# A quarter of the queries takes its softmax maximum from raw scores in SBUF, in a one-core attention and gated-ReLU kernel

## The chip, the cores and the metric

The kernel runs on one core of one Trainium2 chip. Its time is the device time in microseconds (us) of that core; the number compared is the median of several executions.

## The reference

Two blocks read the same input `x` (2048 tokens by 448) and are mixed by one gate per token. All values are float32.

```python
qkv = (x @ wqkv).reshape(B, S, 3, H, Dh)          # H = 16 heads, Dh = 28
scores = einsum("bhqd,bhkd->bhqk", q, k) * (Dh ** -0.5)
a = einsum("bhqk,bhkd->bhqd", softmax(scores, axis=-1), v) ... @ wo
gate = relu(einsum("bsd,df->bsf", x, W_gate)); up = einsum("bsd,df->bsf", x, W_up)
b = einsum("bsf,fd->bsd", gate * up, W_down)       # F = 1792
g = sigmoid((x * gate_w).sum(-1, keepdims=True))
return g * a + (1 - g) * b
```

## The kernel before

The program has three stages. Up to about 144 us it makes q, k and v of all heads (`qk`, L352; `vproj`, L370), with the first products of attention set among them. From there to about 1051 us it runs attention, head by head, with gate and up products of the second block (`gu_mm`, L526) laid among the attention products to fill TensorE. The rest finishes the second block (`down`, L789) and the output projection (`wout`, L744).

A large matmul here streams 512 columns, and float32 operands are split into a high part and a remainder, so that a product of 448 terms is eleven matmuls (`TERMS`). The split is made by `split_f`: ScalarE copies the high part (L130), and GpSimd subtracts it to get the remainder (`pool_low`, L139). Every split chunk of gate and up weights costs ScalarE three copies and GpSimd four subtractions, and the chunk after it is fetched from HBM by a DMA on SyncE's queue (`fetch_f`, L233), which may go only when the buffer of the chunk just split is free.

In attention the scores of a head are made with keys on partitions and 512 queries on the free axis (`scores`, L217), since the product with V needs them that way. ScalarE takes each of these tiles from PSUM through Exp into SBUF (L219). The maximum over keys that is subtracted inside the exponent cannot be read off such a tile, since it would run over partitions. So the kernel computes the scores a second time, with queries on partitions (`smax`, L191), and VectorE reduces each of these tiles to one column (L192). These are called maxima products below: 64 a head, 1024 in all. When the 64 are done, `smax_end` transposes the 16 columns on TensorE (L199), splits them, and two DMAs put them into two spare rows of Q (L207), against which K holds -1. The score matmul of the next head then subtracts its own maximum.

The products with V (`pv`, L560) come in a block of their own at the end of each round: four column-tiled matmuls for each of the key tiles that the round finished, accumulated in one PSUM bank; VectorE then takes the bank to SBUF (L564 for the first block of a head, L566 for later ones, which add). Row sums ride along as a column of ones in V; `row_sums`, `spread` and `normalise` (L574, L582, L586) turn them into a factor and scale the head's output.

The order of instructions is written out by hand. Each string in `ROUNDS` is one round, a letter for each matmul: `s` a score product, `m` a maxima product, `x` a gate or up product (`S`, `M`, `N` are the same with another PSUM bank). What is issued after a round's letters is in the loop's tail: the last gate and up matmuls, the ReLU on ScalarE (L539), the product of gate and up on VectorE (`hidden`, L542), its DMA on GpSimd's queue (L548), the weight splits, `normalise`, and `pv`. Each engine works through its own instructions in this order and waits where it must; eight PSUM banks hold the products until ScalarE or VectorE has read them, so a bank not yet read stops TensorE.

## Time and profile before

| what | before |
| --- | --- |
| median of 3 runs | 1260.16 us (1260.05 to 1260.63) |
| profiled execution, first to last instruction (span) | 1258.2 us |
| PE busy | 1252.8 us |
| VectorE (DVE) busy | 854.8 us |
| ScalarE (ACT) busy | 748.4 us |
| GpSimd (POOL) busy | 374.3 us |

The page gives the profiled execution by its span; no time of its own beside that is listed for it, and the median of the runs is 2.0 us more than the span. PE is TensorE, SPq is SyncE's DMA queue. Overlapping instructions of one engine are counted once in busy time, while the mean in nanoseconds is of one instruction alone, so the pace of instructions that follow each other closely is shorter than that mean. The chain of waits goes back from the last instruction to what released it; in it a matmul has only the time until the next begins, so it shows the pace.

### The profile page before, as it was taken

The numbers are of one execution on the slowest core, as the hardware profiler recorded it, in microseconds if no ns is written. First come the engines' busy times: TensorE is split into PE (matmuls) and PEld (weight loads), VectorE is DVE, ScalarE is ACT, GpSimd is POOL, SyncE is SP. The second block draws the span as 40 slices with busy tenths as digits, with TensorE's granted clock in tenths as the row PEclk, the third lists the DMA queues.
The fourth block names the chain that finished last, engine by engine and source line by source line (L and its number), as shares of the span: only waits on it lengthen the run. The fifth ranks groups of instructions, "written<-read, shape, count | busy, mean of one in ns | idle before, by whom it ended". The sixth has DMA issues, their size and how long they took to land.

```text
span 1258.2 us, 18270 instructions
## 1 busy us (share of the span) xinstructions
PE 1252.8 (100%) x6687; PEld 919.1 (73%) x6687; DVE 854.8 (68%) x1363; ACT 748.4 (59%) x1424; POOL 374.3 (30%) x569
## 2 busy tenths in 40 slices
PE   9999999999999999999999999999999999999998
PEld 6888866677666676666766667766667666899997
DVE  6599767687777797776977778877778224663342
ACT  6312767686666776666866667766677773312121
POOL 4222222312334123423133331134222444651020
PEclk9999999999999999999999999999999999999999
DMA  8955453144245314241544323142431226634432
GB/s 302 315 206 209 117 155 99 50 106 104 60 115 173 81 43 121 68 113 44 130 121 127 100 80 90 43 122 67 114 94 50 84 85 208 223 110 138 145 106 79
DMA packets 54113, 151.00 MB, mean 120 GB/s; under 512 B 10304, under 2 KB 17416, under 8 KB 49160
## 3 DMA queue, kind: packets, MB, share of 16 engines
q1 hardware_dynamic: 36632, 100.44, 29.2%
q0 software_dynamic: 16960, 48.94, 11.0%
q8 instruction: 52, 0.85, 0.3%
q10 hardware_dynamic: 432, 0.46, 0.1%
q14 instruction: 37, 0.30, 0.1%
HBM read 104.16 MB, written 46.03 MB: 119 GB/s over the span
## 4 chain that ended last, share of the span: by engine, by line
PE 99%; DMA 0%; SPq 0%; DVE 0%; ACT 0%; issue 0%
PE b L526 22%; PE b L191 19%; PE b L217 19%; PE b L560 18%; PE b L789 11%; PE b L352 5%; PE b L370 3%; PE b L744 3%; DMA xr<-x 0%; PE b L199 0%; SPq L304 0%; DVE X L136 0%; DVE y L795 0%; ACT X L130 0%; SPq L384 0%
## 5 line engine op out<-in xcount | busy, mean ns | idle before, releaser
L192 DVE TENSOR_REDUCE mx<-b 128x1 f32<-128x512 f32 x1024 | 646.5, 685 | 51.2 <-PE b L191 50.7
L219 ACT ACTIVATE P<-b 128x512 f32<-128x512 f32 x840 | 467.1, 599 | 160.8 <-PE b L217 139.0
L526 PE MATMUL b<-X,wg 128*128 128x512 f32 (+1 forms) x1232 | 415.3, 394 | 0.0
L191 PE MATMUL b<-K,Q 128*128 128x512 f32 x1024 | 389.6, 391 | 0.0
L217 PE MATMUL b<-Q,K 128*128 128x512 f32 x1024 | 389.3, 390 | 0.0
L526 PEld LDWEIGHTS b<-X,wg 128*128 128x128 f32 (+1 forms) x1232 | 220.2, 187 | 53.8 <-issue 9.3
L217 PEld LDWEIGHTS b<-Q,K 128*128 128x128 f32 x1024 | 192.3, 188 | 46.3 <-issue 6.7
L191 PEld LDWEIGHTS b<-K,Q 128*128 128x128 f32 x1024 | 192.4, 188 | 44.3 <-issue 5.9
L560 PE MATMUL b<-P,V 128*32 128x512 f32 x1680 | 188.2, 593 | 0.0
L548 POOL DMA_DIRECT2D h_d<-h x56 | 31.3, 558 | 405.4 <-DVE h L542 354.9
L139 POOL TENSOR_TENSOR wg<-wgr,wg 128x384 fp32r<-128x384 f32 x200 | 143.2, 731 | 10.4 <-DVE wg L133 2.0
L560 PEld LDWEIGHTS b<-P,V 128*32 128x32 f32 x1680 | 52.7, 110 | 120.0 <-issue 116.8
L789 PE MATMUL b<-WD,hh 128*128 128x448 f32 x672 | 138.5, 365 | 0.0
L219 ACT ACTIVATE V<-b 128x512 f32<-128x512 f32 x184 | 105.0, 599 | 48.8 <-PE b L217 42.3
L789 PEld LDWEIGHTS b<-WD,hh 128*128 128x128 f32 x672 | 126.2, 188 | 10.3
L130 ACT ACTIVATE hh<-hr 128x512 fp32r<-128x512 f32 x56 | 35.3, 631 | 124.7 <-PE b L789 120.2
L136 DVE TENSOR_TENSOR hh<-hr,hh 128x512 fp32r<-128x512 f32 x56 | 45.7, 815 | 66.4 <-ACT hh L130 66.3
L352 PE MATMUL b<-X,W 128*128 128x512 f32 x308 | 83.1, 393 | 0.1
L566 DVE TENSOR_TENSOR os<-b,os 128x512 f32<-128x512 f32 x16 | 11.1, 692 | 86.5 <-PE b L560 86.5
L352 PEld LDWEIGHTS b<-X,W 128*128 128x128 f32 x308 | 57.4, 188 | 14.5 <-DVE X L136 1.6
L130 ACT ACTIVATE wg<-wgr 128x384 fp32r<-128x384 f32 x156 | 62.2, 490 | 7.9 <-DMA wgr<-wgu 3.9
L575 POOL DMA_DIRECT2D l_d<-rs x16 | 8.9, 559 | 186.2 <-DVE rs L574 186.2
(74 smaller groups left out, 665.6 us busy)
## 6 DMA issues: line engine op xcount, KB each, us to landing
wgr<-wgu SPq DMA_DIRECT2D x55, 512.0 KB
K<-qk_d SPq DMA_DIRECT2D x64, 224.0 KB
Q<-qk_d SPq DMA_DIRECT2D x64, 224.0 KB
h_d<-h POOLq DMA_DIRECT2D x56, 256.0 KB, 2.7
hr<-h_d SPq DMA_DIRECT2D x56, 256.0 KB
qk_d<-st POOLq DMA_DIRECT2D x21, 512.0 KB, 4.2
x_d<-X POOLq DMA_DIRECT2D x6, 1024.0 KB, 5.4
X<-x_d SPq DMA_DIRECT2D x24, 256.0 KB
```

What stands on the lines that cost most here:

```text
L130: nc.scalar.activation(dst, src, AF.Copy)
L136: nc.vector.tensor_tensor(dst, src, f32(high), op=OP.subtract)
L139: nc.gpsimd.tensor_tensor(dst, src, f32(high), op=OP.subtract)
L191: nc.tensor.matmul(ps, Q[h][:, u * P:(u + 1) * P], K[h % 3][:, c * TB:(c + 1) * TB], start=True, stop=True)
L192: nc.vector.tensor_reduce(MX[h][:, 4 * u + c:4 * u + c + 1], ps, axis=AX.X, op=OP.max)
L217: nc.tensor.matmul(ps, K[h % 3][:, kt * P:(kt + 1) * P], Q[h][:, j * TB:(j + 1) * TB], start=True, stop=True)
L219: nc.scalar.activation(PT[i][:, j], ps, AF.Exp, scale=SCALE)
L352: nc.tensor.matmul(ps, W[:, a, c * P:(c + 1) * P], xf(tb, b), start=(n == 0), stop=(n == NT - 1))
L370: nc.tensor.matmul(ps[:, :VC], xf(tb, b)[:, t * P:(t + 1) * P], W[:, a, 2 * D:2 * D + VC], start=(n == 0), stop=(n == NT - 1))
L526: nc.tensor.matmul(ps, WS[i][rows, s, a], xf(i // NF, b)[rows], start=(n == 0), stop=(n == NT - 1))
L560: nc.tensor.matmul(po[32 * j:32 * j + 32], V[:, h // 4 % 2, i % NK, h % 4], p[:, j], start=(i == i0), stop=(i == i0 + ni - 1))
L789: nc.tensor.matmul(ACC[i // NF][t][:, :D], HH[i][:, a, t * P:(t + 1) * P], WD[:, f, b], start=(f == 0 and n == 0), stop=(f == NF - 1 and n ...
```

## The change

For heads 1 to 15 the last 512 of the 2048 queries no longer get maxima products: 48 of 64 remain for each of these heads (head 0 keeps its 64). The score products of that quarter are made a head earlier, without a maximum in Q's spare rows, and go raw into SBUF (`raw_scores`: ScalarE, Copy instead of Exp). Sixteen raw tiles of a head are folded by VectorE with an elementwise maximum into one running tile (`raw_max`, 15 for each head). `raw_top` finds the maximum over partitions: a 32x32-block transpose, a reduction, four small copies, a second reduction and transpose, all on VectorE; then a DMA writes 512 numbers to HBM and a second reads them back to all 128 partitions, both on SyncE's queue. `raw_less` subtracts that tile from each of the 16 raw tiles (GpSimd; VectorE in two late rounds), and `raw_exp` is the Exp, from SBUF to SBUF on ScalarE.

The raw tiles need room for 24 tiles of 128x512. They take it from V: all of V is written to HBM at the start (`v_d`), and each head's V comes back in a DMA of its own (`load_v`). A round is now always eight key tiles, half a head, so there are 32 rounds, and `pv` always covers eight key tiles, in bank 3. The strings name banks outright (`m0` is a maxima product in bank 0) and have new letters: `r` a raw score product, `d` a `raw_max`, `e` a `raw_exp`. In the strings AA the eight `r` have no `d`, so that the `raw_max` of such a round stand in the loop's tail. Even rounds (first half of a head) are of the kind AA, odd ones BB (two chunks of gate and up) or BA (one chunk). 54 chunks instead of 50 are worked off in attention, and 96 instead of 112 maxima products stand in the first stage.

The strings were all rewritten; one of each shows the form.

```diff
-TWO = ("msMxsxmsxmNxxsmMsxxsmSsxmxsMNxmxsmxsxMSsmxmsxMSmssxmMxSmssxmSxMsxsmxmsxMsxmsxmsMxsmxsxmsxmsxxsmxsmxs"
-       "xmsxmxsxmxsmxsxxmsmshh")
-ROUNDS = [(FIRST, 4)] + [(TWO, 4), (THREE, 4), (ONE, 4)] * 7 + [(LATE, 6), (FINAL, 6)]
+AA = ("xm0s1r2xm6s7xxm3s1xm0xs2r6xm7s3xxm1s0xr2em6xs7xm3s1exm0xs2xr7em3s1xxm0s2exm7xs3xr1em0s2xxm7s3exm1s0x"
+      "r2xem3s1xm0xes2xm3s1xr0xm2s3xm1xs0xm2s3xr1m0s2xm1xs0xm2xs1x")
+BA = ("xm0s1r2m6s7xm3s1xm0s2r6xem7s3m1s0xr2dem6s7xm3s1xem0s2dxm6s7xem3s1m0s2xm7es6xm1s3xr2em0xr6s7m3em1s2xd"
+      "s0m6s3exm7s1xm2s0xr6r3xm7s1r2m0s6xm7xs1s0m2")
+ROUNDS = [FIRST, SECOND, AA, BB, AA, BA, AA, BA] + [AA, BB, AA, BB, AA, BA, AA, BA] * 2
+ROUNDS += [AA, BA, AA, BA, AY, BY, AZ, BZ]
...
+    def rows_of(h):
+        return NK if h == 0 else NK - 4
+    MAXIMA = [(h, u, c) for h in range(H) for u in range(rows_of(h)) for c in range(4)]
...
+    def raw_scores(i, ps, late=False):
+        h, kt = divmod(i, NK)
+        own = prob(i, 3)
+        nc.tensor.matmul(ps, K[h % 3][:, kt * P:(kt + 1) * P], Q[h][:, 3 * TB:], start=True, stop=True)
+        if late:
+            nc.vector.tensor_copy(own, ps)
+        else:
+            nc.scalar.activation(own, ps, AF.Copy)
+    def raw_max(i):
+        run = piece(RUN)
+        nc.vector.tensor_tensor(run, prob(i, 3), run if i % NK > 1 else prob(i - 1, 3), op=OP.max)
+    def raw_top(h):
+        run, turned = piece(RUN), piece(TURNED)
+        nc.vector.transpose(turned, run)
+        top, four = run[:, :16], run[:32, 16:80].rearrange("p (a b) -> p a b", a=4)
+        square, row = run[:32, 96:128], run[:32, 128:160]
+        nc.vector.tensor_reduce(top, turned.rearrange("p (b i) -> p b i", i=32), axis=AX.X, op=OP.max)
+        for a in range(4):
+            nc.vector.tensor_copy(four[:, a], top[32 * a:32 * a + 32])
+        nc.vector.tensor_reduce(square[:, :16], four.rearrange("p a b -> p b a"), axis=AX.X, op=OP.max)
+        nc.vector.transpose(row, square)
+        nc.sync.dma_start(mr_d[h], row[:16])
+        nc.sync.dma_start(piece(TOP), mr_d[h].rearrange("b c -> (b c)").rearrange("(a t) -> a t", a=1).to_broadcast([P, TB]))
+    def raw_less(i, engine):
+        own = prob(i, 3)
+        engine.tensor_tensor(own, own, piece(TOP), op=OP.subtract)
+    def raw_exp(i):
+        own = prob(i, 3)
+        nc.scalar.activation(own, own, AF.Exp, scale=SCALE)
...
+    def load_v(h):
+        VH[h] = fe.tile([P, NK, 32], F32, name=f"v_{h}", tag="v", bufs=2)
+        nc.sync.dma_start(VH[h], v_d[h])
...
+        if r % 2 == 0:
+            small_things(h)
+            if h:
+                for i in range(i0, i0 + 8):
+                    raw_less(i, nc.gpsimd)
...
+        while top < raw:
+            raw_max(top)
+            top += 1
+        if r % 2 and raw == NK * (h + 2):
+            raw_top(h + 1)
+            top += 1
+        if r % 2 == 0 and h:
+            ahead = "e" not in ROUNDS[r + 1]
+            for i in range(i0 + 8, i0 + NK):
+                raw_less(i, nc.vector if ahead else nc.gpsimd)
+                if ahead:
+                    raw_exp(i)
         while summed:
             normalise(summed.pop())
-        for a in {i0, max(i0, (i0 + ni) // NK * NK)}:
-            n = min(i0 + ni, (a // NK + 1) * NK) - a
-            if n > 0:
-                pv(a, n, ps_p if late else ps_m)
-        i0 += ni
+        pv(i0, 8, banks[3])
```

Three places show what the tail of a round now holds. The first is VectorE at the end of a round with a `normalise`, before the change; L542 is `hidden`, L586 `normalise`, L564 the bank of the products with V, and L192 the first maximum of the next round.

```order
L195 TENSOR_REDUCE m_2323<-mx_1887 128x16
L542 TENSOR_TENSOR h_2334<-b_74,rl_2332 128x512
L542 TENSOR_TENSOR h_2342<-b_76,rl_2340 128x512
L586 TENSOR_TENSOR os_1728<-os_1728,rb_2262 128x512
L564 COPY os_2415<-b_71 128x512
L192 TENSOR_REDUCE mx_2421<-b_72 128x1
```

VectorE at the end of an even round after the change. L611 is `hidden`, L267 `raw_max` (its running tile lies in V's space), L659 `normalise`, L637 the bank of the products with V, L229 the maxima of the next round.

```order
L611 TENSOR_TENSOR rl_2432<-b_74,rl_2432 128x512
L611 TENSOR_TENSOR rl_2439<-b_76,rl_2439 128x512
L267 TENSOR_TENSOR V<-P_1072,P_1030 128x512
L267 TENSOR_TENSOR V<-P_1114,V 128x512
L267 TENSOR_TENSOR V<-P_1149,V 128x512
L267 TENSOR_TENSOR V<-P_1197,V 128x512
L267 TENSOR_TENSOR V<-P_1248,V 128x512
L267 TENSOR_TENSOR V<-P_1280,V 128x512
L267 TENSOR_TENSOR V<-P_1331,V 128x512
L659 TENSOR_TENSOR os_1982<-os_1982,rb_2328 128x512
L637 COPY os_2506<-b_72 128x512
L229 TENSOR_REDUCE mx_2378<-b_69 128x1
```

Seven `raw_max`, each of which reads two tiles in SBUF, now stand between `hidden` and the bank of the products with V.

GpSimd around the end of the same even round, from the DMAs of `spread` (L655) on; before the change the remainders (L139) were followed by the DMAs of `normalise` alone.

```order
L139 TENSOR_TENSOR wg_2346<-wgr_2021,wg_2346 128x384 x2
L139 TENSOR_TENSOR wg_2346<-wgr_2021,wg_2346 64x128 x2
L139 TENSOR_TENSOR wg_2356<-wgr_2031,wg_2356 128x384 x2
L139 TENSOR_TENSOR wg_2356<-wgr_2031,wg_2356 64x128 x2
L588 DMA o_d<-os_1728 28x512 x4
L139 TENSOR_TENSOR mh_2419<-mr_2418,mh_2419 16x128
```

After the change; L617 is the DMA of the gate and up product, L149 the remainders of a weight chunk, L285 `raw_less`, L661 the DMAs of `normalise`.

```order
L655 DMA rb_2328<-l_d_103 32x512 x4
L617 DMA h_d_2435<-rl_2432 128x512
L617 DMA h_d_2442<-rl_2439 128x512
L149 TENSOR_TENSOR wg_2444<-wgr_2181,wg_2444 128x384 x2
L149 TENSOR_TENSOR wg_2444<-wgr_2181,wg_2444 64x128 x2
L285 TENSOR_TENSOR V<-V 128x512 x8
L661 DMA o_d<-os_1982 28x512 x4
L149 TENSOR_TENSOR mh_2510<-mr_2509,mh_2510 12x128
```

Eight subtractions of 128x512 have come in behind the remainders, and they stand beside the `raw_max` of VectorE.

SyncE's queue at the end of an odd round, after the change: L303 fetches weight chunks, L280 and L281 are the two DMAs of `raw_top`, L626 is `load_v`, L205 to L212 are K and Q of a later head.

```order
L303 DMA wgr_2181<-wgu 128x1024
L303 DMA wgr_2191<-wgu 128x1024
L280 DMA mr_d_87<-V 16x32
L281 DMA V<-mr_d_87 128x512
L626 DMA v_2239<-v_d 128x512
L205 DMA K_128<-qk_d 28x2048 x4
```

The two DMAs of `raw_top` are new, and they stand behind the fetches that wait for GpSimd's remainders.

216 lines of the change are left out of this document (113 added, 103 removed).

## The prediction

> **What bounds the kernel now.** I read the page's busy times first, then the chain of waits, then the groups, and last the timeline of one round's end.
>
> ```profile
> PE 1252.8 (100%) x6687; PEld 919.1 (73%) x6687; DVE 854.8 (68%) x1363; ACT 748.4 (59%) x1424; POOL 374.3 (30%) x569
> ...
> PE 99%; DMA 0%; SPq 0%; DVE 0%; ACT 0%; issue 0%
> ```
>
> TensorE is the bound without a gap, so a matmul taken out is time saved at its pace, as long as nothing new stops TensorE. The chain gives the paces:
>
> ```profile
> by line: PE b L526 21.8%; PE b L191 18.6%; PE b L217 18.6%; PE b L560 17.7%; PE b L789 10.8%; PE b L352 5.4%; PE b L370 2.9%; PE b L744 2.8%; DMA xr<-x 0.4%; PE b L199 0.3%; SPq L304 0.1%; DVE X L136 0.1%; DVE y L795 0.1%; ACT X L130 0.1%;
> ...
> 316.59 8.72 PE b L560 x80
> ...
> 394.92 9.58 PE b L560 x88
> 404.50 0.21 PE b L199
> ...
> L191 PE MATMUL b<-K,Q 128*128 128x512 f32 x1024 | 389.6, 391 | 0.0
> ```
>
> 18.6% of 1258.2 us over 1024 maxima products is 0.2285 us each (the group's mean of 391 ns overlaps the next matmul). The 80 matmuls of L560 are ten key tiles, 0.87 us each, so eight take 6.97 us. In that block TensorE hands nothing to VectorE and ScalarE, which catch up. What they do there is the question, so here is the block from 394.92 on, with VectorE, GpSimd, ScalarE and SyncE's queue in turn.
>
> ```profile
> 394.71 0.22 DVE L195 TENSOR_REDUCE m<-mx 128x16 f32<-128x64 f32 x1
> 395.45 1.29 DVE L542 TENSOR_TENSOR h<-b,rl 128x512 f32<-128x512 f32 x2 [0.52 <-ACT rl L539]
> 396.66 0.68 DVE L586 TENSOR_TENSOR os<-os,rb 128x512 f32<-128x512 f32 x1
> 404.62 0.69 DVE L564 COPY os<-b 128x512 f32<-128x512 f32 x1 [7.28 <-PE b L560]
> ...
> 396.44 1.14 POOL L548 DMA_DIRECT2D h_d<-h  x2 [5.24 <-DVE h L542]
> 397.60 6.03 POOL L139 TENSOR_TENSOR wg<-wgr,wg 128x384 fp32r<-128x384 f32 x8
> ...
> 394.81 1.09 ACT L539 ACTIVATE rl<-b 128x512 f32<-128x512 f32 x2
> 395.77 2.39 ACT L130 ACTIVATE wg<-wgr 128x384 fp32r<-128x384 f32 x6
> ...
> 400.66 3.32 SPq L233 DMA_DIRECT2D wgr<-wgu  x2
> ```
>
> VectorE sits idle for 7.28 us of it, while GpSimd works until 403.63. Two 128x512 VectorE instructions fill 1.29 us, a pace of 0.60; two ScalarE ones 1.09, a pace of 0.48.
>
> **What two SBUF inputs cost beside GpSimd.** `raw_max` reads two SBUF tiles. Attention has few such instructions now, so I looked where the last stage has them: VectorE and GpSimd about 1102 us, then about 1067 us.
>
> ```profile
> 1102.22 0.69 DVE L136 TENSOR_TENSOR hh<-hr,hh 128x512 fp32r<-128x512 f32 x1
> 1102.83 1.35 DVE L133 CAST WD<-wdr 128x448 fp32r<-128x448 f32 x1
> 1104.42 2.56 DVE L136 TENSOR_TENSOR hh<-hr,hh 128x512 fp32r<-128x512 f32 x1 [0.24 <-ACT hh L130]
> ...
> 1102.39 1.54 POOL L139 TENSOR_TENSOR WD<-wdr,WD 128x448 fp32r<-128x448 f32 x1 [5.58 <-DMA hr<-h_d]
> 1103.90 2.54 POOL L139 TENSOR_TENSOR on<-or,on 128x1024 fp32r<-128x1024 f32 x1
> 1106.39 1.60 POOL L139 TENSOR_TENSOR WD<-wdr,WD 128x448 fp32r<-128x448 f32 x1
> ...
> 1066.76 4.60 DVE L136 TENSOR_TENSOR wg<-wgr,wg 128x384 fp32r<-128x384 f32 x1
> ...
> 1067.54 1.17 POOL L139 TENSOR_TENSOR WO<-wor,WO 128x448 fp32r<-128x448 f32 x1
> 1068.65 1.17 POOL L139 TENSOR_TENSOR WD<-wdr,WD 128x448 fp32r<-128x448 f32 x1
> 1069.76 1.17 POOL L139 TENSOR_TENSOR WO<-wor,WO 128x448 fp32r<-128x448 f32 x1
> ```
>
> The same `hh` takes 0.69 us alone and 2.56 when it meets GpSimd's 2.54 us subtraction: it ends at 1106.98, about half a microsecond after that one. GpSimd's 448-column subtraction takes 1.17 alone and 1.60 when it comes second. So the two take turns, one whole instruction each. At 1066.76 it was worse: VectorE's instruction waited out three subtractions. The L542 pair above has one input in PSUM and keeps its pace.
>
> By the Trainium skill's page "SBUF — State Buffer", section "Who interferes with whom", a VectorE instruction with two SBUF inputs and a GpSimd instruction that reads SBUF exclude each other, and the second to issue waits until the first is done. The rows about 1102 us agree (2.56 us behind 2.54); by this rule the sum is the one with turns below. The 4.60 us row goes beyond it, and by that row the sum would be the second rival's.
>
> **The change, part by part.** Further durations:
>
> ```profile
> L139 POOL TENSOR_TENSOR wg<-wgr,wg 128x384 fp32r<-128x384 f32 x100 | 98.6, 1008 | 2.8 <-DVE wg L133 1.7 <-ACT wg L130 0.5
> L139 POOL TENSOR_TENSOR wg<-wgr,wg 64x128 fp32r<-64x128 f32 x100 | 45.3, 454 | 7.7 <-DVE wg L133 0.3
> L130 ACT ACTIVATE hh<-hr 128x512 fp32r<-128x512 f32 x56 | 35.3, 631 | 124.7 <-PE b L789 120.2 <-DMA hr<-h_d 4.6
> ...
> h_d<-h POOLq DMA_DIRECT2D x56, 256.0 KB, 2.7
> ...
> rb<-l_d POOLq DMA_DIRECT2D x64, 64.0 KB, 2.2
> ```
>
> *Removed on TensorE.* 1024 maxima products become 784: 240 by 0.2285 is 54.8 us saved. Score products stay 1024 and V products eight matmuls a key tile. Six more pairs of half-height gate and up matmuls are worth under 1 us; I leave them out.
>
> *The end of an even round.* Let 0 be the start of the V products. As in the rows, VectorE is done with the two L542 at 1.8, and GpSimd starts the remainders at 2.7. Behind L542 now stand seven `raw_max`, `normalise` and the bank's copy. Each `raw_max` needs the one before it, so alone they take about 0.72 each: 1.8 + 7 x 0.72 + 0.7 gives 7.5, the copy (no second SBUF input) 8.2. TensorE first needs bank 3 again after 6.97 us, a 0.2 us transpose and seven (BA next) or nine (BB next) matmuls, at 8.8 or 9.2. Alone, it fits by a hair. But GpSimd has four remainders (BA) or eight (BB), about 1.0, 1.0, 0.45, 0.45 a chunk, and then eight `raw_less`, about 1.28 each (0.454 plus 384 columns at (1.008 - 0.454)/256 us). Two `raw_max` get in before them, ending at 3.2; from there the engines take turns. BA: four remainders and four `raw_max` to 8.9, `raw_less` 10.2, `raw_max` 10.9, `raw_less` 12.1, `normalise` 12.8, copy 13.55. BB: 13.0. TensorE waits 4.8 or 3.8 us. Rounds 2 to 26 have eight ends of the first sort and five of the second: 38.4 + 19 = 57.4 us. The ends: nothing, if the turns go VectorE's way; 171 us, if GpSimd keeps its run (second rival). I take the turns, because the rows about 1102 us are 128-partition instructions of this size meeting in both orders.
>
> *The end of an odd round.* After BB, one `raw_max` is left; it ends at 2.5, `raw_top` has no two-input instruction, and nothing is late. After BA, five are left. With one L542 done at 1.2 and remainders from 1.9, they end by turns at 7.6. The transpose has no row; between the 0.22 us of the small L195 and the 2.56 us above I take 0.7, a full-width one, then a 0.7 reduction, four small copies that wait for remainders until about 10.1, and 0.4: copy of the bank at 11.2 against a need at 9.0. That is 2.2 us, eight times: 17.6 us. Bounds: 0, and 8 x 6 = 48 if the copies wait out the whole run.
>
> *The tile of maxima comes back.* SyncE's queue is serial. Its second fetch waits for the last remainder (above: second of two issues ending at 403.98, 9.1 us after the block began). `raw_top`'s write stands behind it, at about 10.9 (BA) or 9.2 (BB). Two landings follow; no row gives SyncE's, so I use 2.5, between the 2.2 and 2.7 above. The tile is there at 15.9 or 14.2, the first `raw_less` done 1.3 later. The first `e` of AA stands behind 25 matmuls, 5.7 us into the round: 14.9 or 12.7. It is late by 2.3 or 2.7 us; later ones are spaced 1.37 against 1.28 and do not catch up much. ScalarE is in order, so score tiles queue behind it; six PSUM banks hide about half: 13 x 1.2 = 16 us, between 0 and 33.
>
> *ScalarE.* 231 more instructions of 0.48 to 0.52. A BA round has 24 Exp, 8 copies and 8 `raw_exp`: 32 x 0.48 + 8 x 0.52 = 19.5 us beside 76 matmuls, 17.4. The 2.1 us over fall into the waits above, so I count nothing; without that cover it is 8 x 2.1 = 17 us.
>
> *The rest.* `d` inside BB and BA meets the `raw_less` still running, about two per round by up to 1.3 us; VectorE has 24 x 0.60 + 7 x 0.7 = 19.3 of 21.8 us there, so nothing counted, 30 us at most. The last heads (two-input subtractions on VectorE, ScalarE at 19.5 us in a round of 15.4): 3 us, up to 8. `load_v` reads 256 KB a head ahead; 0. The first stage passes 16 maxima products to FIRST; 0.
>
> Sum: -54.8 + 57.4 + 17.6 + 16 + 3 = +39.2. The profiled span of 1258.2 becomes 1297.4; the median of the runs stands 2.0 above the span, so about 1300 us.
>
> **Rivals.**
>
> *The cover holds, and the kernel is faster.* The place is the end of the even rounds. If the seven `raw_max` run at about 0.72 there, no bank is late and only the tile's return and ScalarE remain. 1260.2 - 54.8 + 16 + 3 + 0 to 17 gives 1224 to 1241, and 1206 if these hide as well. For it: 8.2 is before 8.8, VectorE's idle 7.28 us is real, and `hh` at 1102.22 kept 0.69 while GpSimd waited. Against it: 1.35 and 2.56 when GpSimd was first. It decides at 54.8/13 = 4.2 us of TensorE's waiting per even end, all causes together.
>
> *GpSimd keeps its run.* As at 1066.76, VectorE gets in only when the eight `raw_less` are over. From 3.2: remainders 2.9 or 5.8, `raw_less` 10.2, then five `raw_max`, `normalise` and the copy at 0.7: 21.2 or 24.1. Waits of 12.4 and 14.9 give 8 x 12.4 + 5 x 14.9 = 174 in place of 57.4: about 1416. Against it: at 1102.83 and 1104.42 VectorE got in between two subtractions.
>
> *ScalarE becomes the bound instead,* with VectorE never late: 17 us in BA, 4 in the last heads, the `e` waits in full, 33: 1260.2 - 54.8 + 54, about 1259, no change.
>
> That the products do not disappear is excluded by the order.
>
> **How the numbers follow.** Changes within 0.2% are about what a measurement of this kernel cannot tell from none. Turns: 0.49, from 1262 to 1345 by its own bounds. Cover holds: 0.33, 1206 to 1255. GpSimd's run: 0.13, 1345 to 1420. ScalarE at 1259: 0.05, half of it within 0.2%. So faster 0.35, same 0.03, slower 0.62. The range takes in most of the first rival and a part of the second, 1222 to 1360.
>
> **What would show it.** Right: TensorE idle after each even round's V products, about 4 us, released by VectorE's copy of bank 3; `raw_max` means well over 1 us; POOL subtractions beside them stretched; ScalarE's first `raw_exp` in AA waiting for GpSimd. Wrong: TensorE busy at 99% with a span near 1205, or `raw_max` at 0.7 us. The sum fails if VectorE's place in the turns is better or worse than one for one, or if GpSimd is not yet in its subtractions when `raw_max` starts.

## The result, and the profile after

The changed kernel takes 1592.14 us (median of 4 runs, 1591.37 to 1593.19) where the kernel before takes 1260.11 (1259.86 to 1260.63). The ratio is 1.263, with a 95% interval of 1.2612 to 1.2648. The forecast was 1300 us, 1222 to 1360: slower was right, the size was not.

First the page of the changed kernel: its span, its busy times, and two costly groups on VectorE and GpSimd.

```profile
span 1589.6 us, 18655 instructions
...
PE 1320.9 (83%) x6447; PEld 906.4 (57%) x6447; DVE 1142.1 (72%) x1477; ACT 840.1 (53%) x1655; POOL 699.1 (44%) x817
...
L267 DVE TENSOR_TENSOR V<-V 128x512 f32<-128x512 f32 x115 | 210.8, 1833 | 2.4
...
L285 POOL TENSOR_TENSOR P<-P,V 128x512 f32<-128x512 f32 x116 | 144.8, 1277 | 59.1 <-DMA V<-mr_d 59.1
```

The span grew by 331.4 us. TensorE's time without work went from 5.4 us (1258.2 less 1252.8) to 268.7 (1589.6 less 1320.9), so 263.3 us are waiting. The other 68.1 us are a surprise: TensorE is busy longer, although 240 products, 54.8 us, are gone. By busy time the products left cost 122.9 us more than before (68.1 and 54.8). In the kernel before, the record of one product lasts 0.39 us and the next begins after 0.23, so a wait of up to some 0.16 us leaves no idle time and is counted as busy too.

What TensorE waited for (engine, line, releaser: us in all, times, longest):

```profile
PE b L228 <- DVE os L637: 154.9, 13, 13.0
PE b L228 <- DVE os L639: 26.7, 8, 3.7
PE b L259 <- ACT P L253: 25.3, 6, 5.0
PE b L228 <- ACT P L253: 8.8, 10, 1.8
PE b L228 <- DMA wgr<-wgu: 8.2, 1, 8.2
PE b L251 <- DVE os L637: 7.9, 2, 5.1
PE b L824 <- ACT on L140: 5.5, 1, 5.5
PE b L228 <- DMA Q<-z_d: 4.5, 3, 1.6
PE b L251 <- ACT mr L247: 4.5, 1, 4.5
```

The first row is the place of the forecast: the 13 ends of even rounds, where the bank's copy (L637) is late. Each costs 11 to 13 us. One of them in the timeline of VectorE and GpSimd, at the end of round 2:

```profile
254.48 14.99 DVE L267 TENSOR_TENSOR V<-V 128x512 f32<-128x512 f32 x4
269.38 0.68 DVE L659 TENSOR_TENSOR os<-os,rb 128x512 f32<-128x512 f32 x1
269.99 0.68 DVE L637 COPY os<-b 128x512 f32<-128x512 f32 x1
...
252.01 6.42 POOL L149 TENSOR_TENSOR wg<-wgr,wg 128x384 fp32r<-128x384 f32 x7
258.39 9.79 POOL L285 TENSOR_TENSOR P<-P,V 128x512 f32<-128x512 f32 x8
```

Four `raw_max` take 14.99 us. The chain of waits has the third of them alone:

```profile
258.15 10.60 DVE V L267
```

It lasts 10.6 us, right through GpSimd's eight `raw_less`, which end at 268.18. GpSimd isn't slowed at all: eight in 9.79 us. Most `raw_max` are not slow: the median of the 115 above is 0.69 us, and the mean of 1.83 comes from a few that waited like this one. The two engines do not take turns there. GpSimd finishes its stretch, and then VectorE goes on.

The extra cost of the products shows in the same place, in stretches of the trace (from:to, length, busy us and instructions of PE, weight loads, VectorE, ScalarE, GpSimd, then the granted TensorE clock):

```profile
240.00:255.00 15.00, 14.88 (x100) 8.12 (x100) 11.52 (x14) 9.66 (x19) 6.91 (x11) 1.00 0.16 54
255.00:270.70 15.70, 2.74 (x18) 1.62 (x10) 15.60 (x7) 1.84 (x4) 13.38 (x13) 0.73 0.22 67
270.70:275.60 4.90, 4.88 (x12) 3.83 (x13) 3.08 (x5) 2.59 (x6) 3.09 (x7) 0.50 0.23 51
275.60:295.00 19.40, 19.22 (x85) 14.09 (x83) 16.51 (x27) 17.36 (x34) 0.00 (x0) 1.00 0.00 0
```

After the 13 us of waiting TensorE runs 4.9 us at half its clock: 12 products, about 0.43 us apart where 0.23 is normal. Over the whole run the granted clock is 0.908 instead of 1.000. By the Trainium skill's page "TensorE: Matmul & The Clock Gate", section "Part 1: The HAM clock gate", an idle window of about 3.4 us halves the clock, and about as much steady work brings it back. The rows fit this: after 13 us without work come 4.9 us at half clock, more than one such window and less than two.

Last, the way of the maxima tile, on SyncE's queue after round 3, and the first instructions that wait for it on GpSimd and ScalarE:

```profile
304.11 0.37 SPq L280 DMA_DIRECT2D mr_d<-V  x1
307.86 0.33 SPq L281 DMA_DIRECT2D V<-mr_d  x1
308.28 0.38 SPq L626 DMA_DIRECT2D v<-v_d  x1
308.72 1.69 SPq L205 DMA_DIRECT2D K<-qk_d  x4
...
312.33 4.95 POOL L285 TENSOR_TENSOR P<-P,V 128x512 f32<-128x512 f32 x4 [8.00 <-DMA V<-mr_d]
...
313.62 0.63 ACT L289 ACTIVATE P<-P 128x512 f32<-128x512 f32 x1 [5.00 <-POOL P L285]
```

From the write to the first `raw_less` it is 8.2 us, and everything behind on the queue (V, K and Q of later heads) starts after it.

### The profile page after: what moved, and what is told of

Read it like the earlier page. It is cut to its first block, busy times and chain, and to the rows that moved or that the text cites. A ratio compares the mean times of both kernels' runs of the same rounds, so it can differ in the third digit from the quotient of the medians.

```text
span 1589.6 us, 18655 instructions
## 1 busy us (share of the span) xinstructions
PE 1320.9 (83%) x6447; PEld 906.4 (57%) x6447; DVE 1142.1 (72%) x1477; ACT 840.1 (53%) x1655; POOL 699.1 (44%) x817
## 4 chain that ended last, share of the span: by engine, by line
PE 43%; DVE 24%; ACT 18%; DMA 10%; issue 3%; POOL 1%; SPq 0%; DVEq 0%; POOLq 0%; ACTq 0%
DVE V L267 19%; PE b L595 9%; ACT P L253 9%; PE b L869 8%; PE b L228 7%; PE b L251 6%; PE b L422 4%; PE b L633 3%; DMA V<-mr_d 3%; ACT V L289 3%; ACT P L289 2%; PE b L824 2%; PE b L440 2%; DMA mr_d<-V 2%; DMA Q<-z_d 2%
## 5 line engine op out<-in xcount | busy, mean ns | idle before, releaser
L229 DVE TENSOR_REDUCE mx<-b 128x1 f32<-128x512 f32 x784 | 525.3, 687 | 221.9 <-PE b L228 217.7
L228 PE MATMUL b<-K,Q 128*128 128x512 f32 x784 | 336.8, 432 | 208.1 <-DVE os L637 154.9
L251 PE MATMUL b<-Q,K 128*128 128x512 f32 x784 | 336.9, 433 | 18.6 <-DVE os L637 7.9
L228 PEld LDWEIGHTS b<-K,Q 128*128 128x128 f32 x784 | 159.9, 205 | 277.0 <-DVE os L637 160.4
L617 POOL DMA_DIRECT2D h_d<-rl x56 | 31.6, 565 | 443.4 <-DVE rl L611 434.1
L633 PE MATMUL b<-P,v 128*32 128x512 f32 x1800 | 226.2, 594 | 0.0
L267 DVE TENSOR_TENSOR V<-V 128x512 f32<-128x512 f32 x115 | 210.8, 1833 | 2.4
L149 POOL TENSOR_TENSOR wg<-wgr,wg 128x384 fp32r<-128x384 f32 x216 | 180.5, 850 | 9.2 <-DVE wg L143 0.6
L285 POOL TENSOR_TENSOR P<-P,V 128x512 f32<-128x512 f32 x116 | 144.8, 1277 | 59.1 <-DMA V<-mr_d 59.1
L267 DVE TENSOR_TENSOR V<-P,V 128x512 f32<-128x512 f32 x100 | 150.5, 1505 | 1.6
L285 POOL TENSOR_TENSOR V<-V 128x512 f32<-128x512 f32 x108 | 135.4, 1283 | 29.0 <-DMA V<-mr_d 29.0
L633 PEld LDWEIGHTS b<-P,v 128*32 128x32 f32 x1800 | 61.7, 110 | 144.5 <-issue 144.5
L869 PEld LDWEIGHTS b<-WD,hh 128*128 128x128 f32 x672 | 127.6, 190 | 16.1 <-POOL WD L149 5.7
L259 PE MATMUL b<-Q,K 128*128 128x512 f32 x240 | 103.1, 437 | 25.6 <-ACT P L253 25.3
L633 PE MATMUL b<-V,v 128*32 128x512 f32 x248 | 110.1, 593 | 0.0
```

The costliest lines, as they stand in the source:

```text
L149: nc.gpsimd.tensor_tensor(dst, src, f32(high), op=OP.subtract)
L228: nc.tensor.matmul(ps, Q[h][:, u * P:(u + 1) * P], K[h % 3][:, c * TB:(c + 1) * TB], start=True, stop=True)
L229: nc.vector.tensor_reduce(MX[h][:, 4 * u + c:4 * u + c + 1], ps, axis=AX.X, op=OP.max)
L251: nc.tensor.matmul(ps, K[h % 3][:, kt * P:(kt + 1) * P], Q[h][:, j * TB:(j + 1) * TB], start=True, stop=True)
L259: nc.tensor.matmul(ps, K[h % 3][:, kt * P:(kt + 1) * P], Q[h][:, 3 * TB:], start=True, stop=True)
L267: nc.vector.tensor_tensor(run, prob(i, 3), run if i % NK > 1 else prob(i - 1, 3), op=OP.max)
```

## The experiments

A time without a range beside it is one execution; where there is a ratio to the kernel before, its interval stands with it. Line numbers of some runs are one or two higher than the changed kernel's.

### Where VectorE waits for GpSimd

**No `raw_less`.** Both loops that issue it are left out.

```diff
-                for i in range(i0, i0 + 8):
-                    raw_less(i, nc.gpsimd)
...
-                raw_less(i, nc.vector if ahead else nc.gpsimd)
```

> The subtraction of the maximum (all 240 raw_less) is left out: raw_exp works on raw scores. Theory (GpSimd's stretch): raw_max is slow only because GpSimd's eight raw_less follow each other without a break. Without them the 13 waits at bank 3 after even rounds (11.4 and 13.1 us each, 157 in all) fall to 1 to 4 us each (what the remainders still cost), the ScalarE waits for the maximum's return go too, TensorE's mean granted clock rises from 0.908 to at least 0.97, and the time is about 1320 us (1290 to 1345). Rival (raw_max is dear by itself: two SBUF tiles in V's and K's old places, each waiting for the one before it): the raw_max at even ends keep means over 1.5 us, the waits stay above 8 us each and the time above 1480 us.

Measured: 1446.96 us, granted clock 0.950. TensorE's waits:

```profile
PE b L228 <- DMA Q<-z_d: 54.1, 11, 8.3
PE b L228 <- DVE os L637: 26.9, 13, 3.2
```

At bank 3 the theory holds: 154.9 became 26.9, at most 3.2 each, and the longest `raw_max` 2.8 us instead of 10.6, though nothing about `raw_max` itself had changed. The total missed (1290 to 1345 us were expected), since a wait that the others had hidden came out, 54.1 us for the Q of two heads on.

**`raw_less` behind `normalise`.** The same work, GpSimd's second eight later (the code is shortened).

```diff
-        if r % 2 == 0 and h:  (the raw_less of i0 + 8 to i0 + 15)
         while summed:
             normalise(summed.pop())
+        if r % 2 == 0 and h:  (the same loop)
```

> The eight raw_less of an even round's end are issued behind normalise and its four o_d DMAs, so they run in the first 14 us of the odd round. Theory (GpSimd's stretch): the wait at bank 3 falls to 1.4 us (BA next) and 3.5 us (BB next), but the first raw_max inside BB and BA, about 5 us into the round, now meets the stretch and is kept out until it ends, with the maxima's reductions queued behind it: a new TensorE wait of 5 to 6 us in each of these 13 rounds, now released by VectorE's L229 or L267 rather than by the bank's copy. Time about 1530 us (1490 to 1560). Rival (VectorE is simply overfull in the V products' 7 us, with raw_max, normalise and the copy): moving GpSimd's work out of that block frees it and nothing new appears: about 1430 us.

Measured: 1556.5 us. TensorE's waits:

```profile
PE b L228 <- DVE mx L229: 81.7, 14, 6.9
PE b L228 <- DVE os L637: 27.7, 13, 3.2
```

The wait went where GpSimd's stretch went, into the odd round, released by VectorE's maxima. The 13 waits are 4.0 to 6.9 us each, where 5 to 6 were expected. A VectorE that is only overfull in the block of V products is ruled out.

**What lets VectorE in.** Four runs put something between the `raw_less` of an even round's end.

```diff
 e3  +  nc.gpsimd.memset(pad[:, :1], 0.0)                                     # behind each raw_less
 e5  +  nc.scalar.activation(prob(i, 3)[:, :1], prob(i, 3)[:, :1], AF.Copy)   # ahead of each raw_less
 e8  +  nc.gpsimd.tensor_tensor(pad[:64, :1], pad[:64, :1], pad[:64, 1:2], op=OP.subtract)         # behind
 e11 +  nc.gpsimd.tensor_tensor(pad[:, :1], prob(i, 3)[:, :1], prob(i, 3)[:, 1:2], op=OP.subtract)  # behind
```

> Behind each raw_less at an even round's end GpSimd gets a one-column memset of a spare tile: nothing else is changed, all work stays. Theory (what keeps VectorE out is that GpSimd's subtractions overlap, the next beginning before the one before it has ended; where something stands between two of them VectorE got in): VectorE gets one instruction in at each break, the last raw_max ends after about five raw_less instead of eight, the waits at bank 3 fall from 11.4 and 13.1 us to about 5, and the time to about 1480 us (1450 to 1520). Rival (GpSimd holds the port until its whole queue of SBUF work is done, whatever stands between): the waits stay at 11 to 14 us and the time at 1592 to 1600.

> Ahead of each raw_less at an even round's end ScalarE writes one column of the same tile onto itself, so that each of GpSimd's eight raw_less carries a wait of its own for ScalarE, one that is over long before it is reached. Nothing else changes. Theory (VectorE gets in only where GpSimd's stream leaves a gap, and a wait, even one already met, makes that gap, as the semaphore rows between the remainders do): VectorE gets one turn at each raw_less, the waits at bank 3 fall from 11.4 and 13.1 us to about 5, and the time to about 1490 us (1450 to 1530). Rival (a met wait leaves no gap; only an unfinished one does): 1592 within 8 us, waits as before.

> Behind each raw_less at an even round's end stands a subtraction of one column on 64 partitions of a spare tile. The memset and the met wait in that place did not let VectorE in; the remainders of 64 partitions did, each time. Theory (what lets VectorE in is GpSimd's change to an instruction of 64 partitions, which leaves a gap of 0.08 us): VectorE gets a turn at each raw_less, the waits at bank 3 fall from 11.4 and 13.1 us to about 5, time about 1490 us (1450 to 1530). Rival (it was the semaphore instructions around the remainders, or something else about them): waits as before, 1588 to 1600.

> Behind each raw_less at an even round's end stands a one-column subtraction that reads what this raw_less has just written, so GpSimd must wait there for the end of its own instruction before it. The remainders at which VectorE got in have such a wait for GpSimd itself. Theory (GpSimd's instructions run into each other without giving VectorE a turn until one must wait for the end of the one before it): VectorE gets one instruction in behind each raw_less, waits at bank 3 fall from 11.4 and 13.1 us to about 5, time about 1490 us (1450 to 1530). Rival (GpSimd gives no turn before its SBUF work is out, and the remainders are special for another reason): waits of 12 to 14 us, 1595 to 1615.

Measured: 1588.49, 1591.39, 1605.92 and 1518.69 us. The theories of the first three failed. The memset's rows are typical of the first three: VectorE's one instruction lasts through all eight subtractions.

```profile
256.53 10.84 DVE L267 TENSOR_TENSOR V<-V 128x512 f32<-128x512 f32 x1
...
256.77 1.25 POOL L285 TENSOR_TENSOR P<-P,V 128x512 f32<-128x512 f32 x1
257.97 0.09 POOL L771 MEMSET pad<- 128x1 f32 x1
258.03 1.25 POOL L285 TENSOR_TENSOR P<-P,V 128x512 f32<-128x512 f32 x1
```

And where GpSimd reads what it has just written:

```profile
254.69 7.54 DVE L268 TENSOR_TENSOR V<-V 128x512 f32<-128x512 f32 x4
262.15 0.68 DVE L660 TENSOR_TENSOR os<-os,rb 128x512 f32<-128x512 f32 x1
...
258.61 1.25 POOL L286 TENSOR_TENSOR P<-P,V 128x512 f32<-128x512 f32 x1
259.94 0.52 POOL L772 TENSOR_TENSOR pad<-P 128x1 f32<-128x1 f32 x1
260.43 1.25 POOL L286 TENSOR_TENSOR P<-P,V 128x512 f32<-128x512 f32 x1
261.76 0.53 POOL L772 TENSOR_TENSOR pad<-P 128x1 f32<-128x1 f32 x1
```

Between 258.61 + 1.25 and 259.94 there is a gap of 0.08 us, and a `raw_max` slips in: the one-column instruction then takes 0.52 us instead of 0.19, since it waits for it. The four `raw_max` take 7.54 us instead of 14.99, and the 13 waits fall from 154.9 to 75.4, 5.5 or 6.0 each. These are the turns of the forecast, forced. A memset and a wait that was over long before do not force them; the 64-partition instruction let VectorE in only ahead of the last of the eight. The last run differs from the 64-partition one in its partitions as well as in its wait; an independent one-column instruction on 128 partitions was not run.

The remainders fit in part. This is GpSimd's order with its waits (`Pool` is GpSimd's own semaphore), one chunk:

```
L149 TENSOR_TENSOR wg_8_2173<-wgr_8_1918,wg_8_2173 128x384 [waits DMAHW7_49,PE_49,Activation_49]
L149 TENSOR_TENSOR wg_8_2173<-wgr_8_1918,wg_8_2173 128x384 [waits Activation_49]
L149 TENSOR_TENSOR wg_8_2173<-wgr_8_1918,wg_8_2173 64x128 [waits Activation_49,Pool_49]
L149 TENSOR_TENSOR wg_8_2173<-wgr_8_1918,wg_8_2173 64x128
```

In the changed kernel's trace VectorE got in ahead of the third, which waits for GpSimd itself, and not ahead of the second. It also got in ahead of the fourth, which has no such wait, so a wait for itself is one way to open GpSimd's stretch and not the only one. What holds in the attention of the changed kernel is the gap, by all boundaries between two GpSimd subtractions at which a VectorE instruction with two SBUF inputs was waiting. Where the next subtraction starts before the one before it has ended, VectorE stayed out 154 times in 157; where there is a gap, it got in 72 times in 72. In other runs it also got in where there was no gap: 13 times ahead of the last 64-partition instruction, 13 times ahead of the one subtraction that follows the `raw_less` behind `normalise`, and 14 times behind the one-column subtractions that wait. A gap was always enough, and not always needed.

### What the waiting does to the clock

**Zero products in the waits.** `pad` holds zeros; the products add nothing to the gate accumulator.

```diff
+                if fill and ps is banks[3]:          # fill: 54 in BB, 47 in BA
+                    for _ in range(fill):
+                        nc.tensor.matmul(units[-1][2][:16], pad, xf(0, 0), start=False, stop=False)
+                    fill = 0
                 smax(m, ps)
```

> Where TensorE will wait for bank 3 after an even round, 47 (BA next) or 54 (BB next) matmuls with zero weights are added into an open gate accumulator ahead of the waiting product: 10.7 and 12.3 us of work inside waits of 11.4 and 13.1, so TensorE stays busy and adds nothing. Theory (the wait costs twice, since after it TensorE runs at half its granted clock for some 5 us, 11 matmuls 0.43 us apart instead of 0.23): 13 x 2.4 = 31 us less, about 1561 us (1550 to 1572), mean granted clock about 0.96. Rival (the half clock costs nothing, because VectorE and ScalarE are what limits the round right after a wait): 1592 within 5 us.

Measured: 1573.2 us (1571.8 to 1581.09), ratio 1.2498 (1.246 to 1.2536).

The span and its clock, and then the wait at bank 3:

```profile
core 0: 1572.8 us, clock 0.967
```

```profile
PE b L229 <- DVE os L638: 8.5, 13, 0.8
```

So 646 products more make the kernel 19 us faster, by keeping TensorE's clock up. It is less than the 31 expected and more than nothing: about 1.5 us an end, not 2.4. In its trace the distances between product starts at half pace come to 30 us less than in the changed kernel's, so the clock gave about what was expected, and 11 us of it were lost again elsewhere. That VectorE and ScalarE, which have work to catch up after a wait, take these 11 us is likely and not shown.

### Keeping the two apart

**Other stretches for `raw_max` and `raw_less`.** As the run behind `normalise`, with the strings' `d` and `e` moved. The rows give positions in place of the strings; they count the round's products.

```diff
 AA: e at 25..66, no d             ->  e at 42..84 (every 6th), d at 80, 84, 88, 92
 BB: e at 18..60, d at 23..91      ->  e at 24..66, d at 57..87 (every 5th)
 BA: e at 14..55, d at 20, 28, 52  ->  e at 24..66, d at 57..73 (every 4th)
```

> All work stays, but VectorE's raw_max and GpSimd's raw_less are put in different stretches: the second eight raw_less behind normalise and its DMAs, the raw_max of BB and BA only from the 57th product of the round on, four raw_max of AA in its last 16 products, raw_exp from the 42nd product of AA and the 24th of BB and BA. Theory (GpSimd's stretch is the cause, and it does no harm where VectorE has nothing with two SBUF inputs): waits at bank 3 after even rounds under 1.5 us each, no new ones at the maxima; what is late next is the Q of two heads on, 50 to 70 us of waits for its DMA, and the ends after BA (about 30). Time about 1395 us (1350 to 1440). Rival (VectorE has too much work whatever the order): waits for VectorE's reductions and copies of together over 100 us, time over 1480 us.

Measured: 1452.07 us, clock 0.954. TensorE's waits:

```profile
PE b L228 <- DMA Q<-z_d: 60.0, 11, 6.4
PE b L251 <- ACT P L253: 17.8, 22, 3.9
PE b L228 <- DMA Q<-qk_d: 13.6, 3, 6.2
```

The 13 waits for VectorE's copy after even rounds are gone (0.7 us of that row is left), with all work kept; two waits for it under another product, 8.0 us in the first and the last heads, stay. The time is above the range: Q is late by 73.6 us in all, and half-clock time follows these waits too.

**SyncE's queue.** On top of it (the code is shortened):

```diff
-        if h and h + 2 < H:  load_k(h + 2), load_q(h + 2)        # at an even round's start
+        if r % 2 and h + 3 < H:  load_k(h + 3), load_q(h + 3)    # at an odd round's end, ahead of its fetches
+        if r % 2:  the last raw_max and raw_top                  # also ahead of its fetches
```

> As the run with the two kinds of work apart, and on SyncE's queue the loads of K and Q for two heads on come at the end of the odd round ahead of its fetches and of the maximum's write, not behind them, and an odd round's last raw_max, raw_top and the maximum's write come ahead of the fetches. Theory (Q is late because its loads stand on SyncE's queue behind the maximum's write, whose landing the queue waits out): the waits for Q's DMA, 50 to 70 us in the run before, fall under 12, and ScalarE's waits for the maximum shrink: about 60 us less than that run, 1335 us (1290 to 1375). Rival (Q is late because the transfer itself is slow beside the others, wherever it is issued): the same time as the run before within 15 us.

Measured: 1359.35 us, clock 0.982: 92.7 us less, where about 60 were expected. The longest rows of TensorE's waits:

```profile
PE b L251 <- ACT P L253: 29.5, 20, 4.5
PE b L228 <- DMA wgr<-wgu: 8.2, 1, 8.2
```

Q's row is down to 0.7. The transfers had not been slow; their turn on the queue had come late. After round 3 above, SyncE waited 3.4 us for the landing of the maxima's write before it went on. The run put the loads ahead of the weight fetches too, so what these add is not told apart.

**Later `raw_exp`.** From the 50th product in AA, and the last heads' `raw_less` on GpSimd with `e` in BY and BZ (positions again).

```diff
 AA: e at 42..84  ->  50..89
 BY, BZ: no e     ->  e at 16..51 and 16..58;  AZ: e at 23..60  ->  28..63
```

> The run with the two kinds of work apart and SyncE's queue in the new order, and on top raw_exp in AA from the 50th product of the round on instead of the 42nd, and the last heads' raw_less on GpSimd behind normalise, with raw_exp inside BY and BZ, instead of on VectorE ahead of the bank's copy. Theory (what was left there was ScalarE waiting for the maximum, and the bank's copy behind VectorE's raw_less): the waits for ScalarE fall from 30 to about 8 us, the two of 5.2 us in the last heads go, time about 1325 us (1305 to 1345), still slower than before the change. Rival (later raw_exp only move the wait to the V products, which need them): within 10 us of 1359.

Measured: 1352.18 us. The waits for ScalarE in the row above fell from 29.5 to 7.9 us (with 6.5 under another product), and the time fell by only 7: the rival's number. Its mechanism is not what the trace has, since no wait stands before a V product. All waits together fell by 18 us, and TensorE's busy time rose by 10 (1274.1 to 1284.3): the products went slower instead.

### The other half of the change alone

**No raw scores, the new rounds.** Strings with `r` as an ordinary score, `e` as a maxima product, no `d`; 64 maxima rows for every head; no `raw_max`, `raw_top`, `raw_less`.

> Only the change's other half: rounds of eight key tiles of one head, V loaded a head at a time, gate and up products moved as in the changed kernel; but no raw scores: the last quarter's scores are ordinary ones with their own maxima products (1024 again, where raw_exp stood; 112 in the first stage), and no raw_max, raw_top or raw_less. Theory (the loss is all in the raw scores' work): TensorE stays busy, no wait at bank 3, 1262 us (1250 to 1280). Rival (the new rounds themselves cost: K and Q behind load_v on SyncE's queue, bank 3 needed every seventh microsecond, less gate and up work left to cover the last stage): 1300 us or more.

Measured: 1536.82 us (1535.68 to 1537.73), 1.2194 (1.2174 to 1.2215). Both theories missed. The first row of TensorE's waits says why:

```profile
PE b L230 <- DVE mx L231: 110.4, 144, 1.2
```

TensorE waited 144 times, about 0.8 us each, for a maximum to leave a bank, and 54 times more under another product (57.9 us). The granted clock stayed at 0.992 through these 168 us of short waits. My strings had put the extra products into banks that were needed again at once. The run measured that, not V. So the order was written anew, in an even mixture:

```diff
-AA = ("xm0s1s2xm6s7xxm3s1xm0xs2s6xm7s3...")
+AA = ("xs0m2xs1m7xs6m3xs0m2xxs1m7xs6m3...")    # scores in banks 0, 1, 6, maxima in 2, 7, 3
```

> The change's other half alone, as in the run before of this kind (no raw scores, 1024 maxima products), but with each round's products in an even mixture and banks 0, 1, 6 for scores and 2, 7, 3 for maxima, where that run put the extra maxima products at the places of raw_exp, with banks that were needed again at once. Theory (the rounds of eight key tiles and V a head at a time cost next to nothing; that run measured its poor order): no waits for VectorE's reductions beyond 20 us; with the waits of the first and the last stage (10 and 12 us) about 1282 us (1260 to 1310). Rival (with V a head at a time VectorE and the banks cannot keep up with 32 maxima products a round): over 1400 us.

Measured: 1323.66 us (1321.11 to 1325.65), 1.0497 (1.0477 to 1.0518). This half of the change alone costs 63 us, and I had counted it at nothing. TensorE's waits:

```profile
PE b L230 <- DMA wgr<-wgu: 10.2, 1, 10.2
PE b L230 <- DVE mx L231: 7.2, 20, 0.9
PE b L810 <- ACT on L142: 5.0, 1, 5.0
```

The first row is the first round, which now reaches the maxima of head 2 before that head's Q has landed (the row names the weight fetch issued right behind that Q on the same queue). The third is the last stage, which has 88 products fewer, as in the changed kernel. Its length and products in the kernel before and in the changed kernel, by stretches that end about 4 us ahead of the last instruction:

```profile
1051.30:1254.00 202.70, 202.70 (x988) 183.97 (x980) 96.61 (x134) 50.92 (x82) 59.06 (x54) 1.00 0.48 150
```

```profile
1385.60:1585.00 199.40, 188.26 (x909) 169.80 (x902) 88.11 (x114) 44.41 (x66) 57.88 (x53) 0.97 0.44 136
```

Four chunks of gate and up work, 20 us of products, moved into attention, and the last stage got 3 us shorter: TensorE, busy throughout before, now has work for 188 of its 199 us.

**The first round.** Sixteen of its 32 maxima products moved to the second round (both strings rewritten, every other `m` of the first).

> The change's other half alone, in the even mixture, with 16 of the first round's 32 maxima products moved to the second, so that none there is of head 2, whose Q is loaded as late as before the change. Theory (the first round waits 10.3 us for that load, and some 3 us at half clock follow): about 1312 us (1308 to 1316). Rival (the wait only moves into the second round, or TensorE is then held by ScalarE): 1324 within 3 us.

Measured: 1312.0 us (1308.42 to 1317.57), 1.0413 (1.038 to 1.0446). As expected: the load's wait was worth 12 us. From its page:

```profile
PE 1278.5 (97%) x6687; PEld 911.0 (69%) x6687; DVE 883.5 (67%) x1348; ACT 771.0 (59%) x1423; POOL 392.6 (30%) x593
```

In the profiled execution, 54.5 us longer than that of the kernel before (spans of 1312.7 and 1258.2), TensorE is busy 25.7 us longer with the same 6687 products, at a granted clock of 0.996, and idle 28.8 us longer. So about half of what this half of the change still costs is the pace of the products.

**Chunks back into the last stage.** First four BB made BA in the mixture:

```diff
-ROUNDS = [FIRST, SECOND, AA, BB, AA, BA, AA, BA] + [AA, BB, AA, BB, AA, BA, AA, BA] * 2
+ROUNDS = [FIRST, SECOND, AA, BA, AA, BA, AA, BA] + [AA, BA, AA, BA, AA, BA, AA, BA]   # and one BB in the next eight
```

> The change's other half alone, in the even mixture, with four of its five BB rounds turned into BA, so that 50 chunks of gate and up work lie in attention as before the change, and four, 20 us of products, are back in the last stage. Theory (the last stage had used those products to cover its loads and splits: with 88 products less it took 201.4 us against 202.5, with 11 us of waits and a lower clock behind them): attention gets 20 us shorter, the last stage only 2 to 6 us longer, the whole about 1308 us (1302 to 1314). Rival (products cost the same wherever they stand, and the last stage's waits are of its own): 1324 within 3 us.

Measured: 1338.8 us (1338.22 to 1339.61), 1.0624 (1.0606 to 1.0642). This run and the first of the last two below change part of the computation: token blocks now change inside a round, so that the closing products of two chunks read the next block's tokens. It also brought waits for X, 23.1 us, and rounds 8 and 26 took 48 us where such rounds take 32. Only its last stage can be read:

```profile
1122.60:1332.00 209.40, 207.06 (x986) 184.51 (x979) 95.55 (x134) 50.85 (x82) 59.32 (x55) 0.99 0.45 145
```

With the 88 products back it is 10 us longer than the changed kernel's, not 20. Then, on top of the mended first round, the chunks were taken from the last two heads (no `x` in AY and BZ, half of AZ's), where no block changes:

> The change's other half alone with the first round mended (1312 us), and four chunks of gate and up work taken from the last two heads' rounds (all of AY's and BZ's, half... none of BY's and AZ's) and left to the last stage: 50 in attention as before the change, with the token blocks still changing at a round's end. Theory (the last stage used these products as cover): attention about 14 us shorter (20 of products, less what ScalarE then holds up in the two rounds that have none), the last stage 8 us longer as in the run with four BB turned into BA (209.8 against 201.4), the whole 1300 to 1308 us. Rival (no cover in it): 1312 within 3 us.

Measured: 1317.5 us (1308.38 to 1325.87), 1.0455 (1.0402 to 1.0507): no gain. BZ without gate and up work took 28.2 us for 14.3 us of products (32 by 0.2285 and V's 6.97), at a granted clock of 0.76, and the last four rounds together took 99.5 us where they had taken 100.0 with the four chunks. So attention gave back nothing, while the last stage grew by 9 us, from 202 to 211, up to the last instruction. That the last stage lost cover is shown by its length; that moving chunks back gains, is not.

### Everything that helped, together

The run with later `raw_exp`, eight of the first round's maxima products in the second, and fewer chunks in attention, first by BA for BB, then in AY, AZ and BZ.

> The changed kernel with everything that helped: raw_max and raw_less apart, SyncE's order, later raw_exp, four BB turned into BA, and eight of the first round's maxima products moved to the second. Theory (each of the last two edits is worth here what it is worth in the other half alone): 1352 - 16 - 10 = 1326 us (1312 to 1338), still slower than before the change by about 5%, since what raw scores save on TensorE, 55 us, is less than the short waits they bring. Rival (the last two edits are hidden here behind VectorE and ScalarE): 1345 to 1355.

> The changed kernel with everything that helped (raw_max and raw_less apart, SyncE's order, later raw_exp, eight of the first round's maxima products moved to the second) and the same chunks left to the last stage. Theory (raw scores save 55 us of products and bring short waits of VectorE and ScalarE in every round that cost more than they save, so that the time stays above the other half alone): 1322 us (1308 to 1335). Rival (with all waits mended raw scores pay): under 1295 us, below the other half alone.

Measured: 1333.69 us (1330.6 to 1336.79), 1.0581 (1.0561 to 1.0601), and 1332.49 (1330.0 to 1335.53), 1.0579 (1.0559 to 1.0599). The best form of the change that I found is 5.8% slower than the kernel before, and 15 to 20 us slower than the other half alone (1317.5 with the same chunks, 1312.0 at its best), although it has 240 products fewer. In the second of these runs the waits are short and many, the longest row 10.8 us over 29 waits for ScalarE, and come to 43 us in all. They are not the larger part: TensorE is busy for 1280.0 us, 27.2 more than in the kernel before, although 54.8 us of products are gone. So the products left cost 82 us more, at a granted clock of 0.991; what slows them is not shown. Both times lie in the ranges expected, 1312 to 1338 and 1308 to 1335, and the rival of under 1295 us is out; that short waits alone eat up the saving is not shown. No version beat the kernel before.

## Why the prediction was wrong

| term | predicted | shown |
| --- | --- | --- |
| 240 maxima products | -54.8 | 784 instead of 1024, as counted |
| bank 3 after even rounds | +57.4 | 154.9 (13 waits) |
| bank 3 after BA | +17.6 | 26.1 (7 waits of 3.7) and 2.1 under another product, counted in the last heads too |
| the maxima tile's return | +16 | 25.3 + 8.8, the rows of waits for ScalarE; without `raw_less` 0.9 of them is left |
| last heads | +3 | 16.1 (all waits of the last four rounds) |
| K, Q, first and last stage | 0 | 4.5 + 8.2 + 5.5 and smaller |
| pace of the products left | 0 | 122.9 |

**The mechanism was right, its rule was not.** `raw_max` has two SBUF inputs, meets GpSimd, and makes the bank's copy late; the row L228 <- L637 is what the forecast named. `raw_max` means of 1.5 to 1.8 us were a sign of it too, but they came out right by luck: turns would have made many `raw_max` slow, and a few waited for 10.6 us. The sign of stretched GpSimd subtractions failed. The step that failed is in the end of an even round: "from there the engines take turns". I took it from the rows about 1102 us and took the row of 4.60 us at 1066.76 for the exception. It was the rule here: GpSimd's instructions that ran into each other let VectorE in 3 times in 157. The rival "GpSimd keeps its run" had priced this at 12.4 and 14.9 us an end; 11.3 and 13.0 were measured, and I had given it 0.13. With turns forced (e11) an end costs 6.0 and 5.5 us where I had summed 4.8 and 3.8, so the working with turns was near, and the choice between the two rows was the error. Even so that run takes 1518.69 us, far above the range, so this step alone does not make up the miss. By the Trainium skill's page "SBUF — State Buffer", section "Who interferes with whom", the second to issue waits until the first is done; here it waited for eight instructions, and the measurement decides.

Two smaller points of this working: the bound of 171 us for the ends should have been the rival's 174. And the L542 pair, read there as proof that an instruction with one input in PSUM keeps its pace, ended at 396.74, before GpSimd's first subtraction at 397.60, and shows nothing of the kind. The changed kernel does: VectorE's reductions from PSUM (L229) take 690 ns beside GpSimd's subtractions and 687 without.

**The clock had no term.** Every product left was priced at 0.2285 us. After a 13 us wait the next 4.9 us of products cost double, so each long wait should have carried a surcharge. The slower products are the second largest part of the loss, and against the forecast the largest error: 122.9 us without a term, where the even ends were 97.5 us short. With GpSimd's run at its own price the sum came to 1416, still 176 us below the measured time. Not all of the 122.9 us is the clock: half-pace distances between product starts add 69 us over those before, distances of 0.24 to 0.40 us another 25, among which short waits may hide, and the rest is not placed. Nor is all of the 69 recoverable: with the waits filled 30 of them went and the time fell by 19.

**The odd end and the tile's return** were mis-sized. After BA I had 2.2 us, and 3.7 were measured at seven of the eight ends, with GpSimd's pairs of 384-column remainders not yielding either. The tile took 8.2 us for two landings, not 5.0.

**The terms at nothing were not nothing.** "The first stage passes 16 maxima products to FIRST; 0" overlooked that head 2's maxima then come before its Q (8.2 us; in the other half alone 10.2 us, and 12 gained when it was mended). The chunks moved into attention were counted as a wash, and the last stage needed them: 3 us shorter instead of 20. `load_v` itself hides, but K and Q now stand behind the tile's write and the fetches on SyncE's queue, which cost 73.6 us as soon as the waits that hid it were gone. ScalarE at nothing was near right in the changed kernel, because it had cover; in the mended versions the longest row of waits is ScalarE's, of 10.8 us in the last of them.

**`d` inside BB and BA at nothing** was right for the place that GpSimd's stretch has. Moving the stretch there (e2) made it 81.7 us.

**"The cover holds", 1206 to 1255 us,** was out of reach of every version: with the waits at even ends nearly gone, the best form of the change still takes 72 us more than the kernel before (1332.49 less 1259.99).

What is open: what besides a wait for itself opens GpSimd's stretch, as at the fourth remainder and about 1102 us in the kernel before; and how the other half's 52 us, left after the first round is mended, divide between the last stage, short waits in attention, late Q and slower products, and why products go slower at a nearly full granted clock.

## What to carry to other kernels

Before work with two SBUF inputs is given to VectorE, look for unbroken stretches of GpSimd's subtractions beside it and price the whole stretch, not one instruction; in the trace the sign is a GpSimd instruction that starts before the one before it has ended. Give each long TensorE wait a surcharge for the half clock behind it (waits of 13 us brought one here, waits of 0.8 us did not), and look along the serial DMA queues for what a new round trip pushes back. Where two rows of a trace disagree on a rule, find what differs between them before one is called the exception.

## What the runs showed of the hardware that I had not expected

- A VectorE instruction with two SBUF inputs waited 10.6 us through eight GpSimd subtractions of 1.25 us, none of which was slowed. A GpSimd memset between them did not let it in, nor did a wait that was already met, and a 64-partition instruction did so only as the last of eight; an instruction that must wait for GpSimd's own result did, 51 times in 51, through a gap of 0.08 us.
- TensorE ran at half clock for 4.9 us after a 13 us wait, and 646 useless products in such waits made the kernel 19 us faster. In another run 198 TensorE waits of 0.85 us in the mean, 168 us in all, left the granted clock at 0.992.
- Four chunks fewer in the last stage, 20 us of products, shortened it by 3 us.
